# Residual gates and value products before the first output products, and GpSimd instead of SyncE as the issuer of the block-sum copies

## The chip, the cores and the metric

The kernel runs on one core of one Trainium2 chip. The metric is device time in microseconds of one execution. Engines are named as in the profile: PE is TensorE, PEld its weight loads, DVE is VectorE, ACT is ScalarE, POOL is GpSimd, SP is SyncE.

## The reference

An attention with two kinds of keys feeds a gated feed-forward layer. B = 4 batches, H = 8 heads, S = 768 positions, D = 64, blocks of 32 positions; the model width is 512, the inner width 1536.

```python
k_sum = k.reshape(B, H, nb, block, D).max(axis=3)      # one key per block of 32
v_sum = v.reshape(B, H, nb, block, D).mean(axis=3)     # one value per block
scores_l = scale * q @ k.T,  kept where |i - j| < 16
scores_s = scale * q @ k_sum.T + log(32)
a = softmax(concat(scores_l, scores_s))
x = a @ concat(v, v_sum)                               # heads side by side: 3072 x 512
g, val = x @ w_gate, x @ w_val
out = x + sigmoid(x @ w_res) * ((gelu(g) * val) @ w_out)
```

## The kernel before, in words

The work is cut into eight units of 384 rows; unit u is half `u % 2` of batch `u // 2`. A unit's attention is computed at the end of the unit before it, between that unit's output products, so PE has one long hand-written order of instructions.

**Attention.** Heads go in four pairs. `s_step` multiplies keys by queries: a tile of 64 queries meets 128 key rows, which are its own 64 positions, two rims of 16, the 24 block keys, and padding. ACT takes the exponential into `P` (L302, L299), and DVE multiplies `P` by the band mask `maskt` (L306); both factors of that product lie in SBUF. `av_step` multiplies `P` by `vext` (L320), which has the values in the same 128 rows: positions, rims, and in rows 96 to 127 the block means of v. DVE divides by the sum into `xn` (L338, L340). `xt_step` (PE and ACT, unit 0's end only) or `xt_dma` (SP, L350) turns `xn` into `xT`.

**Feed-forward.** For each of twelve slices `fo`, `fo_step` makes `g` and `vv` (L360), ACT the Gelu (L365), DVE the product into `gvT` (L366). They rotate through a PSUM pool of four banks, `ps_mm`, so `vv` of slice n waits until the DVE product of slice n-2 has been read. Then come the gate products `r` (`res_step`, L398, with a tanh on ACT, L401), the output products `f` (`ffn_step`, L408, three row blocks `sub` of twelve slices each), and `end_step` on DVE (L414, L417) with the store on SP (L421). `first_out` is the order of PE's work at the end of unit 0, `mid_out` that of units 1 to 6.

**Weights and the first unit.** POOL issues all loads of the beginning: gate and value weights in pieces, `w_res` (L193), two rims of v (L109, L110), then `w_out` in three pieces of four slices (L198). After these it issues batch 1's `k` and `v` (L103), and six loads of `q_nat`, 128 rows each (L123).

**Preparing the next batch.** In a batch's second unit its successor `nb` is prepared. `vsum_grp` makes block sums of v: twelve PE products into one bank (L258), a DVE copy into `vpart` (L262), four small DMAs of 6 rows each, from `vpart` into rows 96 to 119 of `vsum` (L264). `vsum_bc` then spreads `vsum` over the twelve tiles of `vext`: four POOL copies of three tiles each (L270). `turn_q` turns `q_nat` into `qT`, one DMA transpose on SP for each half batch (L132). SP and POOL each do their instructions in program order, so before the change SP reaches the two transposes behind the four small DMAs. In unit 1 this stands behind slice 4, in units 3 and 5 behind slice 1. In unit 1, `k` of batch 1 is turned by PE, and `k_place` puts reductions and copies on DVE at slices 0 to 3 (L222 to L231).

The later loads of k, v and q on POOL stand behind `pool_after`, a small copy that waits for the last `xT` of the unit, so they move with PE's work. The loads for batch 1 do not: they stand behind the loads of the beginning.

Of the kernel before, what the change touches and what calls it, by code (L numbers as in the profile page):

```python
# [15 lines left out]
def kernel(  # L16
# [11 lines left out]
    nc = tc.nc  # L28
# [14 lines left out]
    NSUB = TU // 128  # L43
# [35 lines left out]
    vsum = [const.tile([128, DM], BF16, name=f"vsum{i}") for i in range(2)]  # L79
# [50 lines left out]
    def turn_q(b, half):  # L130
        cs = slice(half * NSUB, (half + 1) * NSUB)
        nc.sync.dma_start_transpose(out=qT[b % 2][:, cs].rearrange("d c g k -> d (c g) k"),  # L132
                                    in_=q_nat[:, cs].rearrange("p c f -> p (c f)"))

    with tc.manual_schedule():
# [118 lines left out]
        def vsum_grp(b, pool, tag):  # L254
            vs = pool.tile([128, DM], F32, tag=tag, name="vs")
            for i in range(3):
                for g in range(4):
                    nc.tensor.matmul(vs[32 * g:32 * g + 32, :], bgrp[:, i, :],  # L258
                                     vext[b % 2][0:QT, 3 * g + i, :, 0:D],
                                     start=(i == 0), stop=(i == 2), tile_position=(0, 32 * g),  # L260
                                     skip_group_check=True)
            nc.vector.tensor_copy(vpart[:], vs[:])  # L262
            for g in range(4):
                nc.sync.dma_start(out=vsum[b % 2][96 + 6 * g:102 + 6 * g, :],  # L264
                                  in_=vpart[32 * g:32 * g + 6, :])

        def vsum_bc(b, lo, hi, eng):
# [21 lines left out]
        def s_step(u, hp, st, banks=None):  # L289
            if banks:  # L290
                s = [p.tile([128, 512], F32, tag=tag, name="s") for p, tag in banks]
            else:
                s2 = ps_s.tile([128, 2, 512], F32, tag="s", name="s")
                s = [s2[:, hh] for hh in range(2)]
            s_mm(u, hp, [x[:, 0:TU] for x in s])
            P = ppool.tile([128, 2, HT, QT], BF16, tag="P", name="P")
            if banks:
                for hh in range(2):
                    nc.scalar.activation(P[:, hh].rearrange("p t q -> p (t q)"), s[hh][:, 0:TU], AF.Exp,  # L299
                                         scale=scale, bias=bias_t[:])  # L300
            else:
                nc.scalar.activation(P.rearrange("p a t q -> p a (t q)"), s2[:, :, 0:TU], AF.Exp,  # L302
                                     scale=scale, bias=bias_t[:])
            if u:
                Pf = P.rearrange("p a t q -> p (a t) q")
                nc.vector.tensor_mul(Pf, Pf, maskt.unsqueeze(1).to_broadcast([128, 2 * HT, QT]))  # L306
            st["P", hp] = P
# [45 lines left out]
        def new_unit():  # L353
            return {"xn": upool.tile([128, KO, NSUB, 128], BF16, tag="xn", name="xn"),
                    "xT": upool.tile([128, KO, TU], BF16, tag="xT", name="xT")}
# [12 lines left out]
        def mm_tile(name):  # L368
            return ps_mm.tile([128, 512], F32, tag="mm", name=name)
# [24 lines left out]
        def res_step(st, sub):  # L394
            ss = slice(sub * 128, (sub + 1) * 128)
            r = mm_tile("r")
            for ko in range(KO):
                nc.tensor.matmul(r[:], st["xT"][:, ko, ss], w_res[:, ko, :],  # L398
                                 start=(ko == 0), stop=(ko == KO - 1))
            st["th", sub] = work.tile([128, DM], F32, tag="th", name="th")  # L400
            nc.scalar.activation(st["th", sub][:], r[:], AF.Tanh, scale=0.5)  # L401

        def ffn_step(st, gvT, sub, lo, hi):
            ss = slice(sub * 128, (sub + 1) * 128)
            if lo == 0:
                st["f", sub] = mm_tile("f")
            for fo in range(lo, hi):
                nc.tensor.matmul(st["f", sub][:], gvT[:, fo, ss], w_out[:, fo, :],  # L408
                                 start=(fo == 0), stop=(fo == FO - 1), skip_group_check=True)
# [13 lines left out]
        def end_step(u, st, sub):  # L423
            end_part(u, st, sub, st["f", sub], slice(0, DM))
# [28 lines left out]
        st = new_unit()  # L453
# [17 lines left out]
        gvT = upool.tile([128, FO, TU], BF16, tag="gvT", name="gvT")  # L471
# [49 lines left out]
        def first_out(u, st, gvT, nst):  # L521
            n = u + 1
            other = dict(pool=ps_t, tag="t")
            turn = dict(pool=ps_t, tag="t", copy=nc.scalar.copy)
            s_step(n, 0, nst)
            s_step(n, 1, nst, TO2)
            res_step(st, 0)
            res_step(st, 1)
            ffn_step(st, gvT, 0, 0, 4)
            av_step(n, 0, nst)  # L530
            av_step(n, 1, nst, **other)
            s_step(n, 2, nst)
            ffn_step(st, gvT, 1, 0, 4)
            res_step(st, 2)
            ffn_step(st, gvT, 2, 0, 4)
            xt_step(n, 0, nst, **turn)
            av_step(n, 2, nst)
            s_step(n, 3, nst)
            ffn_step(st, gvT, 0, 4, 8)
            ffn_step(st, gvT, 1, 4, 8)  # L540
            xt_step(n, 1, nst, **turn)
            ffn_step(st, gvT, 2, 4, 8)
            av_step(n, 3, nst)
            xt_step(n, 2, nst, **turn)
            ffn_step(st, gvT, 0, 8, FO)
            end_step(u, st, 0)
            ffn_step(st, gvT, 1, 8, FO)
            xt_step(n, 3, nst, **turn)
            ffn_step(st, gvT, 2, 8, FO)
            end_step(u, st, 1)  # L550
            end_step(u, st, 2)
# [36 lines left out]
        def pool_after(x):  # L588
            nc.gpsimd.tensor_copy(gate2[:], x)

        for u in range(NU):
            b, half = u // 2, u % 2
            nb = b + 1
            if half == 0 and nb == 1:
                k_sb[nb] = k_tile()
                load_k(nb, k_sb[nb], 0, 1)
                v_loads(nb)
                load_q_nat(nb)
            if u:
                gvT = upool.tile([128, FO, TU], BF16, tag="gvT", name="gvT")  # L600
            for fo in range(0 if u else 2, FO):
                if u > 1 and fo == 0:
                    fo_first(st, gvT)
                elif u and fo == FO - 2:
                    fo_last_two(st, gvT)
                elif u == 0 or fo < FO - 2:
                    fo_step(st, gvT, fo)
                if u == 0:
                    unit0_extras(fo)
                if u == 0 and fo == 9:  # L610
                    tq = turn_all(q_sb[1])
                if u == 0 and fo in (9, 10):
                    for hp in range(2 * fo - 18, 2 * fo - 16):
                        q_place(1, hp, tq[hp])
                if half == 0 and 1 < nb < B and fo == 0:
                    pool_after(st["xT"][0:1, KO - 1, 0:1])
                    k_nat = load_k_nat(nb)
                    v_loads(nb)
                if half == 0 and b and fo == 1:
                    v_rims(b, HT, NT)  # L620
                if half == 0 and 1 < nb < B and fo == 6:
                    turn_k(nb, k_nat)
                    k_rims(nb, slice(0, NP), nc.gpsimd)
                if half == 1 and nb < B:
                    if fo == 0:
                        v_rims(nb, 0, HT)
                        if nb > 1:
                            pool_after(st["xT"][0:1, KO - 1, 0:1])
                            load_q_nat(nb)
                    if fo == (4 if nb == 1 else 1):  # L630
                        vsum_grp(nb, ps_t, "t")
                        for i in range(4):
                            vsum_bc(nb, 3 * i, 3 * i + 3, nc.gpsimd)
                        turn_q(nb, 0)
                        turn_q(nb, 1)
                    if nb == 1:
                        if fo == 0:
                            tk = turn_all(k_sb[nb])
                        if fo < NP:
                            k_place(nb, fo, tk[fo])  # L640
                    elif 2 <= fo < 2 + NP:
                        k_blocks(nb, fo - 2)
            if u == NU - 1:
                last_out(u, st, gvT)
            else:
                nst = new_unit()
                (mid_out if u else first_out)(u, st, gvT, nst)
                st = nst
# [30 lines left out]
```

## Time and profile before

| | us |
|---|---|
| median of 6 runs | 261.24 |
| lowest and highest run | 260.77, 262.44 |
| the profiled execution, its own time | 262.18 |
| its span (first to last instruction) | 260.3 |
| PE busy | 250.0 |
| DVE busy | 156.7 |
| ACT busy | 126.0 |
| POOL busy | 104.1 |

The profiled execution took 1.88 us more than its span, and it stands 0.94 us above the median. The granted clock of PE was 0.999. Instructions that issue a DMA stand in the timeline of POOL or of SP's queue (SPq); the time to landing runs from the start of the issue. Unit 0 ends with `first_out` from about 40.2 to 55.7 us, unit 1 runs to 73.8 us, and the end of each later unit begins about every 28 to 29 us.

### The profile page before, as it was taken

The numbers are of one execution on the slowest core, as the hardware profiler recorded it, in microseconds if no ns is written. First come the engines' busy times: TensorE is split into PE (matmuls) and PEld (weight loads), VectorE is DVE, ScalarE is ACT, GpSimd is POOL, SyncE is SP. The second block draws the span as 40 slices with busy tenths as digits, with TensorE's granted clock in tenths as the row PEclk, the third lists the DMA queues.
The fourth block names the chain that finished last, engine by engine and source line by source line (L and its number), as shares of the span: only waits on it lengthen the run. The fifth ranks groups of instructions, "written<-read, shape, count | busy, mean of one in ns | idle before, by whom it ended". The sixth has DMA issues, their size and how long they took to land.

```text
span 260.3 us, 5828 instructions
## 1 busy us (share of the span) xinstructions
PE 250.0 (96%) x2306; PEld 138.3 (53%) x2306; DVE 156.7 (60%) x346; ACT 126.0 (48%) x210; POOL 104.1 (40%) x142
## 2 busy tenths in 40 slices
PE   6999987999999999999999999999999999999993
PEld 2565543555645565545654565545654665456543
DVE  5955653479668544677758444778566544854324
ACT  6785357456372535633383437443482337343310
POOL 8895454275080789234440888154530000000000
PEclk9999999999999999999999999999999999999999
DMA  5999999999962999949903999949904400230002
GB/s 82 177 116 180 197 220 195 198 130 196 67 121 48 173 136 139 128 119 167 149 8 64 191 113 145 115 118 172 150 12 114 100 0 3 48 137 0 0 37 86
DMA packets 98299, 29.61 MB, mean 114 GB/s; under 512 B 83384, under 2 KB 95104, under 8 KB 98160
## 3 DMA queue, kind: packets, MB, share of 16 engines
q0 software_dynamic: 68400, 14.96, 70.4%
q1 hardware_dynamic: 29872, 14.29, 24.7%
q8 instruction: 18, 0.29, 0.5%
q14 instruction: 9, 0.07, 0.1%
HBM read 29.36 MB, written 6.29 MB: 137 GB/s over the span
## 4 chain that ended last, share of the span: by engine, by line
PE 75%; DMA 14%; POOL 4%; DVE 3%; SPq 1%; issue 1%; ACT 0%; DVEq 0%
PE f L408 23%; PE g L360 19%; PE vv L360 19%; PE r L398 7%; DMA w_out<-in_moe_w_out_dram 5%; DMA w_gate<-in_moe_w_gate_dram 4%; DMA q_sb<-in_q_dram 3%; PE ao L320 3%; PE s L284 2%; DMA qT<-q_nat 2%; POOL vext L103 1%; POOL w_val L190 1%; POOL w_gate L189 1%; SPq L264 1%; DVE P L306 1%
## 5 line engine op out<-in xcount | busy, mean ns | idle before, releaser
L366 DVE TENSOR_TENSOR gvT<-ge,vv 128x384 bf16<-128x384 f32 x96 | 52.7, 552 | 51.6 <-PE vv L360 46.5
L365 ACT ACTIVATE ge<-g 128x384 f32<-128x384 f32 x96 | 47.1, 491 | 75.0 <-DVE gvT L366 41.4
L360 PE MATMUL g<-xT,w_gate 128*128 128x384 bf16 x384 | 78.8, 326 | 0.7 <-DMA w_gate<-in_moe_w_gate_dram 0.5
L360 PE MATMUL vv<-xT,w_val 128*128 128x384 bf16 x384 | 78.8, 326 | 0.7 <-DMA w_val<-in_moe_w_val_dram 0.7
L408 PE MATMUL f<-w_out,gvT 128*128 128x512 bf16 x276 | 64.9, 380 | 1.1 <-DMA w_out<-in_moe_w_out_dram 1.1
L360 PEld LDWEIGHTS <-w_gate 128*128 128x128 bf16 x384 | 37.1, 98 | 26.9 <-issue 1.6
L360 PEld LDWEIGHTS <-w_val 128*128 128x128 bf16 x384 | 37.2, 98 | 26.3 <-DMA w_val<-in_moe_w_val_dram 2.4
L408 PEld LDWEIGHTS <-gvT 128*128 128x128 bf16 x276 | 25.6, 98 | 30.5 <-DMA w_out<-in_moe_w_out_dram 1.6
L103 POOL DMA_DIRECT2D vext<-in_v_dram x48 | 32.6, 721 | 13.1 <-DMA w_out<-in_moe_w_out_dram 4.7
L401 ACT ACTIVATE th<-r 128x512 f32<-128x512 f32 x24 | 13.6, 606 | 28.4 <-PE r L398 28.4
L270 POOL COPY vext<-vsum 32x1536 bf16<-32x1536 bf16 x12 | 17.1, 1463 | 22.8 <-DMA vsum<-vpart 22.8
L414 DVE SCALAR_TENSOR_TENSOR th<-th,f 128x512 f32<-128x512 f32 (+2 forms) x26 | 16.7, 641 | 15.2 <-PE f L408 15.2
L306 DVE TENSOR_TENSOR P<-P,maskt 128x768 bf16<-128x768 bf16 x28 | 16.9, 605 | 11.8 <-ACT P L302 7.2
L398 PE MATMUL r<-w_res,xT 128*128 128x512 bf16 x96 | 23.2, 380 | 0.7 <-DMA w_res<-in_moe_w_res_dram 0.7
L302 ACT ACTIVATE P<-s,bias_t 128x768 bf16<-128x768 f32 x17 | 15.3, 902 | 7.1 <-PE s L284 6.9
L340 DVE TENSOR_TENSOR xn<-ao,rz 128x384 bf16<-128x384 f32 x32 | 17.8, 557 | 1.1
L417 DVE SCALAR_TENSOR_TENSOR o<-th,xn 128x512 f32<-128x512 f32 (+2 forms) x26 | 17.5, 674 | 1.5 <-DMA out_dram<-o 0.6
L117 POOL DMA_DIRECT2D k_nat<-in_k_dram x24 | 16.4, 745 | 1.1 <-DMA k_nat<-in_k_dram 0.8
L123 POOL DMA_DIRECT2D q_nat<-in_q_dram x18 | 15.9, 919 | 0.8 <-issue 0.7
L299 ACT ACTIVATE P<-s,bias_t 128x384 bf16<-128x384 f32 x30 | 15.7, 579 | 0.3 <-PE s L284 0.3
L222 DVE TENSOR_REDUCE ks<-kW 128x24 bf16<-128x768 bf16 x16 | 15.1, 944 | 0.4 <-ACT kW L237 0.3
L398 PEld LDWEIGHTS <-xT 128*128 128x128 bf16 x96 | 8.9, 98 | 10.6 <-issue 0.7
(82 smaller groups left out, 164.6 us busy)
## 6 DMA issues: line engine op xcount, KB each, us to landing
out_dram<-o SPq DMA_DIRECT2D x23, 256.0 KB, 2.3
vext<-in_v_dram POOLq DMA_DIRECT2D x48, 64.0 KB, 6.5
q_nat<-in_q_dram POOLq DMA_DIRECT2D x18, 128.0 KB, 7.4
w_gate<-in_moe_w_gate_dram POOLq DMA_DIRECT2D x6, 256.0 KB, 9.9
w_val<-in_moe_w_val_dram POOLq DMA_DIRECT2D x6, 256.0 KB, 10.5
w_out<-in_moe_w_out_dram POOLq DMA_DIRECT2D x3, 512.0 KB, 12.6
k_nat<-in_k_dram POOLq DMA_DIRECT2D x24, 64.0 KB, 4.6
vext<-vext SPq DMA_DIRECT2D x6, 144.0 KB, 5.7
```

The costliest lines, as they stand in the source:

```text
L103: nc.gpsimd.dma_start(out=vext[b % 2][0:QT, t, :, 0:D], in_=v[b, :, t * QT:(t + 1) * QT, :].rearrange("h p d -> p h d"))
L117: nc.gpsimd.dma_start(out=k_nat[:, t].rearrange("p (h d) -> p h d", d=D), in_=k[b, :, t * QT:(t + 1) * QT, :].rearrange("h p d -> p h d"))
L270: eng.tensor_copy(vext[b % 2][96:128, lo:hi, :, 0:D], src)
L306: nc.vector.tensor_mul(Pf, Pf, maskt.unsqueeze(1).to_broadcast([128, 2 * HT, QT]))
L340: nc.vector.tensor_mul(xn, ao[:, :, :, 0:D], rz.to_broadcast([128, NSUB, 2, D]))
L360: nc.tensor.matmul(ps[:, 0:TU], w[:, ko, fo * 128:(fo + 1) * 128], st["xT"][:, ko, :], start=(ko == 0), stop=(ko == KO - 1), skip_group_ch ...
L365: nc.scalar.activation(ge[:], g[:, 0:TU], AF.Gelu)
L366: nc.vector.tensor_mul(gvT[:, fo, :], ge[:], vv[:, 0:TU])
L398: nc.tensor.matmul(r[:], st["xT"][:, ko, ss], w_res[:, ko, :], start=(ko == 0), stop=(ko == KO - 1))
L408: nc.tensor.matmul(st["f", sub][:], gvT[:, fo, ss], w_out[:, fo, :], start=(fo == 0), stop=(fo == FO - 1), skip_group_check=True)
L414: nc.vector.scalar_tensor_tensor(th[:, cs], th[:, cs], 1.0, f[:, 0:n], ALU.add, ALU.mult)
L417: nc.vector.scalar_tensor_tensor(o.rearrange("p (k d) -> p k d", d=128), th[:, cs].rearrange("p (k d) -> p k d", d=128), 0.5, x, ALU.mult, ...
```

## The change

Three things are changed.

In `first_out` all three `res_step` stand together, ahead of the value products of head pairs 0 and 1 and the scores of pair 2. The first third of all three output products follows. Before, a third of output product 0 stood behind the second `res_step`, and the third `res_step` between output products 1 and 2.

The four DMAs from `vpart` to `vsum` are issued by POOL instead of SP, for batches 1, 2 and 3.

`turn_q` stands ahead of `vsum_grp` in the program. In unit 1 the block moves from slice 4 to slice 5. On POOL the four DMAs come behind the six loads of `q_nat` and ahead of the four copies; on SP the two transposes now follow the rims of v (L109, L110) directly.

```diff
@@ vsum_grp
             for g in range(4):
-                nc.sync.dma_start(out=vsum[b % 2][96 + 6 * g:102 + 6 * g, :],
+                nc.gpsimd.dma_start(out=vsum[b % 2][96 + 6 * g:102 + 6 * g, :],
                                   in_=vpart[32 * g:32 * g + 6, :])
@@ first_out
             s_step(n, 0, nst)
             s_step(n, 1, nst, TO2)
-            res_step(st, 0)
-            res_step(st, 1)
-            ffn_step(st, gvT, 0, 0, 4)
+            for sub in range(NSUB):
+                res_step(st, sub)
             av_step(n, 0, nst)
             av_step(n, 1, nst, **other)
             s_step(n, 2, nst)
-            ffn_step(st, gvT, 1, 0, 4)
-            res_step(st, 2)
-            ffn_step(st, gvT, 2, 0, 4)
+            for sub in range(NSUB):
+                ffn_step(st, gvT, sub, 0, 4)
             xt_step(n, 0, nst, **turn)
@@ main loop, half == 1 and nb < B
-                    if fo == (4 if nb == 1 else 1):
+                    if fo == (5 if nb == 1 else 1):
+                        turn_q(nb, 0)
+                        turn_q(nb, 1)
                         vsum_grp(nb, ps_t, "t")
                         for i in range(4):
                             vsum_bc(nb, 3 * i, 3 * i + 3, nc.gpsimd)
-                        turn_q(nb, 0)
-                        turn_q(nb, 1)
```

The number of instructions on PE, DVE and ACT is the same before and after.

## Prediction

> **What bounds the kernel now.** First the page, to see whose time counts.
>
> ```profile
> span 260.3 us, 5828 instructions
> PE 250.0 (96%) x2306; PEld 138.3 (53%) x2306; DVE 156.7 (60%) x346; ACT 126.0 (48%) x210; POOL 104.1 (40%) x142
> ```
>
> PE works 250.0 of 260.3 us, and the change takes no work from it. A gain can only come out of PE's pauses, so I looked for those near the edited lines. PE's timeline at the end of unit 0:
>
> ```profile
> 41.43 1.89 PE L398 MATMUL r<-w_res,xT 128*128 128x512 bf16 x8 [0.72 <-DMA w_res<-in_moe_w_res_dram]
> 44.38 1.04 PE L408 MATMUL f<-w_out,gvT 128*128 128x512 bf16 x4 [1.06 <-DMA w_out<-in_moe_w_out_dram]
> 45.35 0.57 PE L320 MATMUL ao<-vext,P 128*64 128x65 bf16 x24
> 45.85 0.35 PE L284 MATMUL s<-qT,kW 64*128 64x64 bf16 x12
> ```
>
> PE stands before the first output product until the first piece of w_out is there. Four r take 0.86 us in the chain, so eight that begin at 41.43 free PE at 43.16, and the pause in issue is 44.38 - 43.16 = 1.22 us (the row's 1.06 counts from the modelled end of the last r).
>
> The second place is the start of the attention for unit 2. The chain of waits there:
>
> ```profile
> 66.47 0.68 DVE vpart L262
> ...
> 69.46 0.66 SPq L264
> ...
> 70.29 3.96 DMA qT<-q_nat
> 74.25 0.04 issue
> 74.29 0.36 PE s L284 x12
> ...
> 75.61 2.34 DVE P L306 x2
> ```
>
> The scores wait for the turned q, whose transposes stood on SP behind four small DMAs, and those behind the copy into vpart. Then two mask products on DVE take 2.34 us. The timelines of DVE and POOL say why:
>
> ```profile
> 75.61 1.86 DVE L306 TENSOR_TENSOR P<-P,maskt 128x768 bf16<-128x768 bf16 x1 [1.04 <-ACT P L302]
> 77.40 0.55 DVE L306 TENSOR_TENSOR P<-P,maskt 128x768 bf16<-128x768 bf16 x1
> 104.40 0.56 DVE L306 TENSOR_TENSOR P<-P,maskt 128x768 bf16<-128x768 bf16 x1 [0.81 <-ACT P L302]
> ```
>
> ```profile
> 71.38 5.70 POOL L270 COPY vext<-vsum 32x1536 bf16<-32x1536 bf16 x4 [9.21 <-DMA vsum<-vpart]
> ```
>
> The same mask takes 0.56 us one unit later, with POOL idle, and 1.86 us here, where the last POOL copy runs until 77.08: it ends 0.4 us after that copy. The table of windows prices the whole, from the time when PE could begin the scores to its eleven-product f group:
>
> ```profile
> 73.84:78.77 4.93, 4.45 (x85) 2.53 (x85) 3.76 (x7) 3.49 (x7) 3.23 (x3) 1.00 0.34 64
> 102.85:106.96 4.11, 4.11 (x85) 2.36 (x85) 2.25 (x6) 3.48 (x7) 0.79 (x2) 1.00 1.74 143
> ```
>
> 4.93 against 4.11 us: 0.82 lost, 0.45 of it before the scores (74.29 - 73.84), 0.37 behind the masks.
>
> **Part one, the order at the end of unit 0.** In the pause go the third r (0.86, to 44.02), two value products (45.35 to 45.85: 0.50, to 44.52) and the scores of pair 2 (0.28, to 44.80). The first f then finds w_out landed (issued 32.37, 12.0 to landing, 44.37). What these need is there: the first two masks begin at 42.38 and 43.32 and take 0.56, so they end at 42.94 and 43.88; the rims of v land at 31.04 + 11.1 = 42.1; the exponentials that free the banks end at 43.28. ACT gets a third tanh (0.60) ahead of the exponential of pair 2, which starts about 44.9 instead of 46.24, for a value product near 47.6. The later pieces of w_out land at 34.35 + 12.6 = 46.95 and 35.67 + 13.8 = 49.47; PE now asks at 49.59 and 52.94, then 1.22 earlier. So unit 1 starts 1.22 us earlier. Cover gone, the price would be the pause again.
>
> **Part two, slice 5 instead of 4.** DVE is busy without pause from 58.8 to 68.1 and follows PE, so it moves 1.22 forward too. The block sums (12 products, 0.76 us from 63.87 to 64.64) used to separate vv of slices 4 and 5. Now vv 5 asks for its bank two groups of 0.65 behind vv 4, at 63.13 - 1.22 + 1.30 = 63.2, while the DVE product of slice 3 frees it at 64.74 - 1.22 = 63.5: about 0.3 us lost. Slice 6 has the sums ahead of it and waits no more. PE can begin the scores of unit 2 at 73.84 - 1.22 + 0.3 = 72.9. vpart, now behind the product of slice 5 (0.55), still ends about 66.4 instead of 67.15: the product of slice 4 ends at 66.02 + 0.54 - 1.22 = 65.3, and two operations follow that overlap a little.
>
> **Part three, the transposes ahead.** They wait for q_nat alone. Its third load has landed at 58.60 + 8.9 = 67.5, and a transpose lands 3.7 to 3.96 after its issue: 71.3 to 71.5. Unit 5's first transpose is issued while loads of q_nat still run and also takes 3.7. PE asks at 72.9, so the 0.45 us is gone, with 1.4 us in hand. The second transpose is for a later unit.
>
> **Part four, the small DMAs on POOL.** POOL idles for 9.21 us there, so the issues cost PE nothing by themselves; what counts is when the copies behind them end. A POOL issue of an SBUF-to-SBUF move takes 0.52 us (L109). Four from 66.45: the last starts at 68.0, ends at 68.5. From SP, the last issue ended at 70.12 and the copies began at 71.38, 1.26 later. The nearest POOL row with nothing ahead of it is a v load of 64 KB, 2.6 us from its start: 70.6. With 1.26 after the end it is 69.8. The four stand behind q_nat, whose last load lands at 61.20 + 8.1 = 69.3, so not earlier. I take 70.2, between the two, as the transfer is small but has loads ahead and the transposes beside it. Lower bound 69.5; upper 71.6, if each issue cost 0.94 like q_nat's (70.2 + 1.26 = 71.5).
>
> The Trainium skill, page "DMA: Bandwidth & Descriptors", section "Issuing engine by pattern", speaks against this part: plain copies belong on Sync, and its specifications give about 1 us to the first byte from GpSimd and 0.6 from Sync. By that page, an estimate, the copies would begin at 70.6 and the gain below would be 0.8.
>
> The copies take 5.70: they end at 75.9 instead of 77.08. PE's scores at 72.9 bring the first mask to DVE at 74.45 (104.40 - 102.85 = 1.55 later), inside the third or fourth copy. Even if it slips in between two copies, the second mask waits for the end of the last. In the trace before, the f group began 1.70 after POOL's end (78.77 - 77.07). So f begins at 75.9 + 1.70 = 77.6, against 78.77: **1.2 us earlier**. PE's own path allows 72.9 + 4.11 = 77.0, so 1.76 is the most.
>
> In batches 2 and 3, SP's small DMAs shared the queues with q_nat; the copies began 0.6 us after q_nat's last landing (unit 5: 177.77 + 6.8 = 184.5, then 185.15). On POOL they are right behind it. POOL ended its copies at s + 1.10 and s + 1.67 (133.01 - 131.91, 190.83 - 189.16), and by the mask rows PE loses only past s + 2.5, so I cost these at nothing. The cover is 1.4 and 0.8 us. All else in these units moves with xT.
>
> Sum: 262.18 - 1.2 = 261.0 for the profiled execution; the same difference on the median gives 261.24 - 1.2 = 260.0, told as 260.1 for small waits unseen.
>
> **The rivals.**
>
> Copies no longer in the way: if they begin by 69.6, PE's own path decides: 1.76 us, 259.5. For it: 1.26 after 68.5 is 69.8, close. Against: q_nat's landing at 69.3, and transposes that now run beside its last loads.
>
> The gain of unit 0 given back: if the copies begin between 70.6 and 71.38, the masks hand back what PE had won, and 0 to 0.78 stays: 260.5 to 261.2, centre 260.9. For it: four issues in a row, into a queue in use. Against: vpart is 0.75 us earlier and SP's four issues took 2.94 us, POOL's should take 2.1.
>
> Slower: the small DMAs, now in POOL's queue behind q_nat, land more than 2 us after it. The place is the masks of units 2, 4 and 6. Copies that begin at 72.4 cost 1.0 in unit 2; the same 1.9 behind the landing of q_nat instead of 0.6 costs 0.5 in unit 6 (1.3 less the cover of 0.8) and nothing in unit 4: 262.7. It decides from a start of 72.2 on, where the loss passes 0.78. For it: q_nat takes 8 us to land here, so this queue is long. Against: the rims from POOL (L109, L110) landed 0.3 to 0.5 us after the load ahead of them (41.8 and 42.1 behind w_res at 41.4).
>
> **How the numbers follow.** About 0.3% (0.78 us) is what a measurement of this kernel can tell from no change. Forecast 0.53; PE's own path 0.13; given back 0.23; slower 0.11. Faster is 0.53 + 0.13 = 0.66, of which 0.02 falls within 0.3%, as the forecast's lower end is near it: 0.64. Slower keeps 0.10, and 0.26 is left for no change. The range runs from 259.4, which takes in PE's own path, to 261.7, past no gain at all (261.24); outside lie most of the slower case, some 0.10, and about 0.05 for terms sized wrongly.
>
> **What would show it.** PE without a pause from r to the first f in unit 0, 12 output products in a row after the scores; unit 1 from about 54.5 us; PE at the scores of unit 2 by 72.9 without waiting for qT; POOL's copies from 70.2 and f about 77.6; the first mask in unit 2 still longer than 0.56; in units 4 and 6 masks of 0.56. The prediction is wrong if the copies begin at 71.4 or later, if masks in units 4 or 6 grow, or if a new wait for a PSUM bank appears at slice 5 that is much over 0.3 us.

## The result, and the profile after

The changed kernel takes 260.42 us (median of 21 runs, 259.78 to 261.44), the kernel before 261.52 (46 runs, 260.47 to 262.58). The ratio is 0.996, with a 95% interval from 0.9948 to 0.9972: faster by about 1.05 us, between 0.73 and 1.36.

The profiled execution of the changed kernel took 260.30 us. Its page begins:

```profile
span 258.4 us, 5826 instructions
PE 250.5 (97%) x2306; PEld 138.9 (54%) x2306; DVE 157.9 (61%) x346; ACT 125.9 (49%) x210; POOL 111.2 (43%) x154
```

The span is 1.9 us shorter, but PE's work is what it was (250.5 against 250.0), so all of it is pauses. Not all of them belong to the change, as the accounts below show. POOL has twelve instructions more: the small DMAs.

PE's timeline at the end of unit 0 (start, length, then what stood before it):

```profile
40.30 2.75 PE L398 MATMUL r<-w_res,xT 128*128 128x512 bf16 x12 [0.47 <-DMA w_res<-in_moe_w_res_dram]
42.98 0.57 PE L320 MATMUL ao<-vext,P 128*64 128x65 bf16 x24
43.76 2.76 PE L408 MATMUL f<-w_out,gvT 128*128 128x512 bf16 x12
...
53.32 0.81 PE L360 MATMUL g<-xT,w_gate 128*128 128x384 bf16 x4
```

The pause between r and f is gone, and f is a row of twelve without a wait. Unit 1 begins 13.02 us behind the first r, against 14.26 before (55.69 - 41.43): 1.24 us less.

The attention for unit 2, first in PE's timeline, then in the chain of waits:

```profile
71.47 0.52 PE L284 MATMUL s<-qT,kW 64*128 64x64 bf16 x24
...
76.36 0.38 PE L320 MATMUL ao<-vext,P 128*64 128x65 bf16 x12 [1.36 <-DVE P L306]
...
77.13 2.55 PE L408 MATMUL f<-w_out,gvT 128*128 128x512 bf16 x11
```

```profile
70.27 0.49 ACT ge L365
...
73.01 3.31 DVE P L306 x2
```

The scores wait for nothing any more: they follow the last vv at once, and SP's step, which stood in the chain, has left it. But the two masks are longer, 3.31 us instead of 2.34, and PE stands 1.36 us before the second half of the `ao` products. The timelines of DVE and POOL show them apart:

```profile
73.01 1.56 DVE L306 TENSOR_TENSOR P<-P,maskt 128x768 bf16<-128x768 bf16 x1 [0.81 <-ACT P L302]
74.50 1.81 DVE L306 TENSOR_TENSOR P<-P,maskt 128x768 bf16<-128x768 bf16 x1
```

```profile
65.71 2.02 POOL L264 DMA_DIRECT2D vsum<-vpart  x4 [3.94 <-DVE vpart L262]
71.29 6.35 POOL L270 COPY vext<-vsum 32x1536 bf16<-32x1536 bf16 x4 [3.56 <-DMA vsum<-vpart]
```

POOL issues the four small DMAs in 2.02 us, as forecast, then stands 3.56 us until the last has landed. The copies begin at 71.29 and lie under both masks, where before they lay under the first alone. The table of windows gives the price: the stretch from the scores of unit 2 to the first g of unit 2, and below it the same stretch for unit 3, where no copies run:

```profile
71.47:85.52 14.05, 12.69 (x146) 6.35 (x145) 10.36 (x18) 7.14 (x11) 7.09 (x7) 1.00 0.26 66
101.21:113.71 12.50, 12.50 (x146) 6.28 (x145) 8.20 (x18) 7.14 (x11) 2.21 (x5) 1.00 1.19 133
```

14.05 against 12.50: 1.55 us are lost here. Before, the same stretch (74.29 to 87.16) took 12.87.

So the two profiled executions differ by four items. The first r begins at 40.30 instead of 41.43 (1.13, the landing of `w_res`, ahead of everything edited); r to the first g of unit 1: 1.24 less; from there to the scores 18.15 instead of 18.60: 0.45 less; from the scores to the first g of unit 2: 1.18 more. The rest, from that g to the end, is 172.88 (258.4 - 85.52) instead of 173.14: 0.26 less. The sum, 1.13 + 1.24 + 0.45 - 1.18 + 0.26 = 1.90, is the difference of the spans. Without the first item, which changes from one execution to the next, 0.77 is left.

### The profile page after: what moved, and what is told of

Same layout as the page of the kernel before. It is cut to its first block, busy times and chain, and to the rows that moved or that the text cites. A ratio compares the mean times of both kernels' runs of the same rounds, so it can differ in the third digit from the quotient of the medians.

```text
span 258.4 us, 5826 instructions
## 1 busy us (share of the span) xinstructions
PE 250.5 (97%) x2306; PEld 138.9 (54%) x2306; DVE 157.9 (61%) x346; ACT 125.9 (49%) x210; POOL 111.2 (43%) x154
## 4 chain that ended last, share of the span: by engine, by line
PE 79%; DMA 12%; POOL 4%; DVE 2%; ACT 1%; issue 1%; POOLq 0%; DVEq 0%
PE f L408 23%; PE g L360 21%; PE vv L360 21%; PE r L398 8%; DMA w_res<-in_moe_w_res_dram 5%; DMA w_val<-in_moe_w_val_dram 3%; DMA q_sb<-in_q_dram 3%; PE ao L320 3%; PE s L284 2%; POOL vext L103 1%; DVE P L306 1%; POOL w_gate L189 1%; PE vs L258 1%; DMA out_dram<-o 1%; POOL w_val L190 1%
## 5 line engine op out<-in xcount | busy, mean ns | idle before, releaser
L360 PE MATMUL vv<-xT,w_val 128*128 128x384 bf16 x384 | 78.8, 326 | 0.5 <-DMA w_val<-in_moe_w_val_dram 0.5
L360 PE MATMUL g<-xT,w_gate 128*128 128x384 bf16 x384 | 78.8, 326 | 0.2
L306 DVE TENSOR_TENSOR P<-P,maskt 128x768 bf16<-128x768 bf16 x28 | 18.1, 648 | 11.5 <-ACT P L302 7.1
L270 POOL COPY vext<-vsum 32x1536 bf16<-32x1536 bf16 x12 | 17.7, 1517 | 13.1 <-DMA vsum<-vpart 13.1
(83 smaller groups left out, 173.1 us busy)
```

Source lines behind the costliest of these rows:

```text
L270: eng.tensor_copy(vext[b % 2][96:128, lo:hi, :, 0:D], src)
L360: nc.tensor.matmul(ps[:, 0:TU], w[:, ko, fo * 128:(fo + 1) * 128], st["xT"][:, ko, :], start=(ko == 0), stop=(ko == KO - 1), skip_group_ch ...
```

## The experiments

All of them compute the whole result. They use one account per profiled execution, in us, with the columns: start of the first r; r to the first g of unit 1; from there to the scores of unit 2; scores to the first g of unit 2 (12.50 where nothing is lost); from there to the end of the span. The last column is the ratio to the kernel before, with its interval.

| run | first r | to unit 1 | to scores | to unit 2 | to end | ratio |
|---|---|---|---|---|---|---|
| before | 41.43 | 14.26 | 18.60 | 12.87 | 173.1 | 1 |
| before again (e8) | 40.31 | 14.34 | 18.23 | 12.88 | 173.1 | - |
| changed | 40.30 | 13.02 | 18.15 | 14.05 | 172.9 | 0.9960 [0.9948, 0.9972] |
| changed again (e7) | 41.14 | 13.02 | 18.15 | 13.63 | 172.9 | 0.9956 [0.9940, 0.9973] |
| order alone (e1) | 40.80 | 13.03 | 18.41 | 12.86 | 173.1 | 0.9957 [0.9937, 0.9976] |
| queues alone (e2) | 40.72 | 14.24 | 18.14 | 13.88 | 172.8 | 1.0015 [0.9996, 1.0033] |
| changed, two copies late (e3) | 41.07 | 13.02 | 18.15 | 12.50 | 172.9 | 0.9946 [0.9926, 0.9966] |
| changed, small DMAs before the transposes (e4) | 40.73 | 13.03 | 21.06 | 12.50 | 172.8 | 1.0049 [1.0028, 1.0070] |
| order alone, two copies late (e5) | 40.58 | 13.03 | 18.51 | 12.49 | 173.5 | 0.9936 [0.9921, 0.9950] |
| changed, SP as issuer (e6) | 40.88 | 13.03 | 18.14 | 14.80 | 178.4 | 1.0136 [1.0108, 1.0163] |
| changed, slice 4 (e9) | 40.68 | 13.03 | 18.14 | 13.60 | 172.9 | 0.9964 [0.9943, 0.9985] |
| before, four more DMAs at the end (e10) | 40.38 | 14.50 | 18.69 | 12.82 | 172.9 | - |

### The two halves: the order alone, the queues alone

The first kernel is before with only the new order in `first_out`; the second is the changed kernel with the old order.

```diff
 e1: before, and of the change only
     first_out:  res_step x3 together, the three first ffn_step together
 e2: the changed kernel without that
```

> Part one alone: the new order of products at the end of unit 0, with the small block-sum DMAs left on SP, behind slice 4 and ahead of the transposes. Theory A (the pause ahead of the first output product is what the change removes, and DVE, the sums and POOL's copies follow PE): everything behind moves together by 1.2 us, so 261.5 - 1.2 = 260.3, about the whole change; PE still waits some 0.4 us for the turned q, and the masks of unit 2 are about as long as before (one of 1.9 us). Rival B (without the queue changes the copies stay where the loads of q put them and the masks hand the gain back): 0.3 to 0.6 us faster, 260.9 to 261.2, with the f group of unit 2 less than 0.6 us nearer to the start of the gate products.

> Parts two to four alone: the transposes ahead, the small DMAs on POOL, the block behind slice 5; the order at the end of unit 0 is the old one. Theory A: the 0.45 us that PE waited for the turned q goes, but the copy into vpart comes no earlier (67.2 to 67.7) and the small DMAs stand behind the first transpose, so POOL's copies begin at 71.5 to 72.2 and the masks take that back: within 0.5 us of before, 261.0 to 262.0. Rival B (the queues bring the gain): 0.8 us or more faster, at most 260.7.

Order alone: 260.30 us, ratio 0.9957, the whole gain of the changed kernel. POOL's and DVE's timelines:

```profile
69.32 5.70 POOL L270 COPY vext<-vsum 32x1536 bf16<-32x1536 bf16 x4 [7.47 <-DMA vsum<-vpart]
```

```profile
73.56 1.86 DVE L306 TENSOR_TENSOR P<-P,maskt 128x768 bf16<-128x768 bf16 x1 [0.86 <-ACT P L302]
```

With the small DMAs on SP the copies begin 28.5 us behind the first r (69.32 - 40.80), with POOL as issuer 31.0 (71.29 - 40.30). The first mask takes 1.86 and the second 0.55, as in the kernel before, and the loss there stays as small as it was (12.86).

Queues alone: 261.83 us, ratio 1.0015, where the interval just takes in no change. The timelines of PE, POOL and DVE:

```profile
73.10 0.52 PE L284 MATMUL s<-qT,kW 64*128 64x64 bf16 x24
```

```profile
72.76 6.35 POOL L270 COPY vext<-vsum 32x1536 bf16<-32x1536 bf16 x4 [3.54 <-DMA vsum<-vpart]
```

```profile
74.64 3.13 DVE L306 TENSOR_TENSOR P<-P,maskt 128x768 bf16<-128x768 bf16 x2 [0.81 <-ACT P L302]
```

The wait for the turned q is gone here too (18.14), and more is lost at the masks (13.88 instead of 12.87). What parts two to four give at q they hand back with interest at the masks. The time is inside what theory A allowed, but the copies begin at 72.76, later than its 71.5 to 72.2, although `vpart` ends at 66.88, before its 67.2.

### Is it the copies under the masks?

If the copies are what costs the 1.5 us, a kernel in which only two of them stand there must lose nothing. The second half of `vext` is needed only from unit 3 on, so copies 3 and 4 of batch 1 can go behind the loads of the next batch's k.

```diff
+                    if nb == 2:
+                        vsum_bc(1, 6, 9, nc.gpsimd)
+                        vsum_bc(1, 9, 12, nc.gpsimd)
...
-                        for i in range(4):
+                        for i in range(2 if nb == 1 else 4):
```

In e3 this is done to the changed kernel, in e5 to the kernel with the order alone, where the small DMAs are still on SP.

> The whole change, and in batch 1 the last two of POOL's four copies, which unit 3 alone reads, stand behind the loads of the next k instead of directly behind the first two. Theory A (what PE waits for in unit 2 is mask products that DVE cannot run while POOL copies): the copies end near 74.2 instead of 77.6, the second mask takes 0.56 us, the f group of unit 2 follows the scores by 4.1 to 4.3 us instead of 5.7, and the time is some 1.3 us below the changed kernel, 259.1. Rival (the masks are late for another reason, such as ACT's exponentials or the DMAs themselves): no change against the changed kernel, 260.4, and masks still over 1 us.

> Part one alone, and the last two of batch 1's four POOL copies behind the loads of the next k; the small DMAs stay on SP and ahead of the transposes. Theory A (part one brings 1.2 us, the masks 0.37, the turned q 0.45, each by itself): the masks no longer wait for the copies, PE still waits for the turned q; the f group of unit 2 follows the scores by 4.1 to 4.2 us and the time is 0.3 to 0.4 us below part one alone, 259.9. Rival (the masks' wait is hidden by something else): as part one alone, 260.3.

The timelines of POOL and DVE in e3:

```profile
71.72 2.87 POOL L270 COPY vext<-vsum 32x1536 bf16<-32x1536 bf16 x2 [3.74 <-DMA vsum<-vpart]
```

```profile
73.78 1.69 DVE L306 TENSOR_TENSOR P<-P,maskt 128x768 bf16<-128x768 bf16 x2 [0.81 <-ACT P L302]
```

POOL is done at 74.59, the first mask takes 1.22 us and the second 0.55, and the stretch is 12.50, with nothing lost: the copies under the masks were the whole loss. In e5 the copies end at 72.09, ahead of the masks, and both take 0.56 in DVE's timeline:

```profile
73.44 0.56 DVE L306 TENSOR_TENSOR P<-P,maskt 128x768 bf16<-128x768 bf16 x1 [0.82 <-ACT P L302]
74.38 0.56 DVE L306 TENSOR_TENSOR P<-P,maskt 128x768 bf16<-128x768 bf16 x1 [0.38 <-ACT P L299]
```

e5 took 259.86 us, ratio 0.9936 [0.9921, 0.9950], e3 259.68, ratio 0.9946 [0.9926, 0.9966]. They are the two fastest kernels of this study, and their intervals overlap, so which is better isn't settled. On one point e3 missed: its account promises 1.1 to 1.5 us over the changed kernel (12.50 against 13.63 and 14.05, with the other columns equal), but 0.3 to 0.4 came by the ratios, 0.7 by the medians (260.42 and 259.68). One profiled execution stands there for a median, and where the rest went is open.

### Why do the copies begin so late?

The four small DMAs were issued by 67.74 and the last landed at 71.24. Theory A says that the transposes, now ahead, hold them back; the rival, that this queue is slow behind the loads of q in any case. In e4 the transposes of batch 1 wait until the small DMAs have landed, by way of a 16-byte DMA on SP that reads `vsum`.

```diff
-                        turn_q(nb, 0)
-                        turn_q(nb, 1)
                         vsum_grp(nb, ps_t, "t")
+                        nc.sync.dma_start(out=scr[:], in_=vsum[1][119:120, 0:8])
+                        turn_q(nb, 0)
+                        turn_q(nb, 1)
```

(in unit 1; batches 2 and 3 as in the changed kernel)

> The whole change, but in batch 1 the two transposes wait, through a 16-byte DMA on SP that reads vsum, until the small DMAs have landed. Theory A (a running DMA transpose keeps the small DMAs of POOL's queue from being served): without a transpose under way the four land within 1.0 us of the last load of q_nat, as they do in units 4 and 6, so POOL's copies begin 0.6 to 1.2 us behind that landing instead of 2.4. PE then waits for the turned q until 73 to 74 us, so the time is 0.3 us faster to 0.5 us slower than the changed kernel. Rival (POOL's issue and its queue are slow by themselves): the copies still begin over 2 us behind q_nat's last landing, and the time is 1.5 us or more above the changed kernel, as the transposes come later too.

POOL's copies and PE's scores:

```profile
70.07 5.70 POOL L271 COPY vext<-vsum 32x1536 bf16<-32x1536 bf16 x4 [2.42 <-DMA vsum<-vpart]
```

```profile
74.82 0.53 PE L285 MATMUL s<-qT,kW 64*128 64x64 bf16 x24 [2.85 <-DMA qT<-q_nat]
```

Without transposes ahead POOL waits 2.42 us behind its last issue instead of 3.56, and the last small DMA takes 2.9 us from the start of its issue instead of 4.0. The DMA view of the same window, 67.3 to 69.4, first of the changed kernel, then of e4 (packets, MB, share; a packet's whole time counts where it starts, so a share can pass 100%):

```profile
q1 hardware_dynamic: 1086, 0.28, 125.6%
q0 software_dynamic: 2, 0.00, 0.1%
```

```profile
q0 software_dynamic: 154, 0.02, 11.1%
```

Queue q1 carries the transposes, q0 what POOL issues. In the changed kernel q0 moves two packets in 2.1 us while the transposes run; without transposes it moves 154. It is a stop and not an even slowing: from 66.4 to 67.3 q0 had moved 310 packets beside 214 of q1, and right after the stop, from 69.4 to 70.0, it moves again although the transposes go on:

```profile
q1 hardware_dynamic: 268, 0.06, 47.2%
q0 software_dynamic: 96, 0.02, 15.9%
```

Of the 24 rows of 1 KB that the small DMAs move, six go by 67.11, none until 69.58, and then 18 within 0.15 us. So in this order the transposes do hold the small DMAs back, for some 1.1 us (2.42 against 3.56). That settles the direction, not all of the size: A expected the copies 0.6 to 1.2 us behind the landing of the last q and the rival over 2; they begin 1.9 behind it (68.13 to 70.07), against 2.4 in the changed kernel. In e4 all 24 rows had moved by 68.4, and fifteen of the sixteen engines had reported the last small DMA done by 68.82, but the last only at 70.02. On one engine an instruction fetch stands in the DMA view in each kernel, here from 66.97 for 1.44 us. That the two are cause and effect wasn't tried.

Nor does every running transpose hold them back. A's expectation takes units 4 and 6 for places without one, but in unit 6 of the changed kernel the first transpose runs from 180.71 to 184.46, and the small DMAs land in the middle of it, by 183.43, 0.94 us behind q. There they had been issued 1.4 to 4.1 us ahead of the transpose; in unit 2 the first is issued within 0.1 us of it and the rest behind it. Whether that order makes the difference wasn't tried.

As a kernel e4 is slower: 262.97 us (nine runs, 261.81 to 263.49), ratio 1.0049 [1.0028, 1.0070]. That is over 1.5 us above the changed kernel, where the rival had it and not A: the scores wait 2.85 us for q, more than A had for it. The copies meet the masks no more (12.50).

### The transposes first, the small DMAs on SP

e6 is the changed kernel with part four undone: SP issues the small DMAs, behind the transposes.

```diff
-                nc.gpsimd.dma_start(out=vsum[b % 2][96 + 6 * g:102 + 6 * g, :],
+                nc.sync.dma_start(out=vsum[b % 2][96 + 6 * g:102 + 6 * g, :],
```

> The whole change but for the issuer: the small DMAs are issued by SP, now behind the two transposes. Theory A (a small DMA behind the transposes lands late, whoever issues it, and the copies decide unit 2): SP issues the four from about 70.5 on, the copies begin at 74.3 to 75.2, after both masks; the masks take 0.56 us, but the first value product waits for the second copy until 77.2 to 78.1, so the f group comes 0.8 to 1.7 us later than in the changed kernel: 261.2 to 262.1. Rival B (only POOL's queue is slow, SP's is not): the copies begin by 72.5 and the time is that of the changed kernel or less, 260.4.

265.58 us, ratio 1.0136 [1.0108, 1.0163]: 3.6 us slower than before. That is the median of four runs, 264.40 to 267.10. SP issues the small DMAs at 69.76 to 72.80 and the copies begin at 74.17, so early that the second mask still meets one (1.51 us instead of the expected 0.56). PE now waits for the copies themselves, in its timeline:

```profile
75.69 0.26 PE L320 MATMUL ao<-vext,P 128*64 128x65 bf16 x5 [0.42 <-POOL vext L270]
77.43 0.48 PE L320 MATMUL ao<-vext,P 128*64 128x65 bf16 x19 [1.49 <-POOL vext L270]
```

The expectation (261.2 to 262.1) counted unit 2 alone. The stretch from scores to g takes 14.80 there, 13.63 in unit 4 and 16.16 in unit 6, against 12.50. If `turn_q` is to stand ahead, the small DMAs must leave SP: part four is what makes part three bearable.

### Does the start of r move the loss? Slice 4 or 5?

e7 and e8 are the changed kernel and the one before, once more; e9 is the changed kernel with the block at slice 4.

> The changed kernel once more, for its time beside the others and for a second profile. Theory A (the start of r, set by the landing of w_res, differs by up to 1.1 us between executions, while the loads of q_nat, and with them the transposes, the small DMAs and the copies, do not move with it): whenever r begins, the f group of unit 2 begins at 77.0 to 77.4, so the distance from r to that f group is 36.8 where r begins at 40.3, and shorter by as much as r begins later. Rival (the distance is fixed by PE and DVE): 36.8 within 0.1 again, whenever r begins.

> The kernel before once more, for a second profile. Theory A (here the small DMAs and the transposes stand behind the copy into vpart, and so behind PE and DVE): the distance from the first r to the f group of unit 2 is 37.3 within 0.2, whenever r begins. Rival (the loads fix it here too): the f group at 78.8 within 0.2, whenever r begins.

> The whole change with the block of unit 1 back behind slice 4. The prediction priced the move to slice 5 at a wait of 0.3 us for a PSUM bank; the changed kernel's trace shows none. Theory A (the bank of that product was free anyway, and the copy into vpart comes between the products of slices 4 and 5, some 0.55 us earlier, in front of small DMAs that wait for the transposes): the same time as the changed kernel within 0.3 us, 260.4 to 261.0, vpart ending about 64.9 and the copies beginning within 0.4 us of 71.3 to 71.7. Rival (the move to slice 5 costs its 0.3 us in a way the trace does not show, or the earlier small DMAs pass the first transpose): 0.5 to 1.0 us faster than the changed kernel, the copies beginning at 70.5 or earlier.

The changed kernel came to 260.73 us again, ratio 0.9956. Its first r began 0.84 us later than in the first profile, the f group of unit 2 only 0.42 later (77.55 against 77.13; the record of its first product is missing, and 77.55 is counted back from the second). So in this kernel half of a late start is made up: the copies follow the loads of q, which follow the loads of the beginning, and a PE that comes later meets them less (the copies begin 0.60 us ahead of the scores instead of 0.18, and the stretch is 13.63 instead of 14.05). That lies between the two theories. In the kernel before, with r at 40.31, the stretch from the scores was the same as with 41.43 (12.88 and 12.87); the wait for q was 0.37 smaller. From r to the f group it took 37.06 (40.31 to 77.37, counted back in the same way), a little outside theory A's 37.3 within 0.2 and far from the rival, which had f at 78.8.

Slice 4: 260.24 us, ratio 0.9964, account as in e7. Part two is worth nothing that shows.

### A quarter of a microsecond at the end

From the first g of unit 2 to the end, the changed kernel is 0.25 us shorter with the same instructions on PE. What SP waits for at the very end, in the view of waits (line, releaser: total, count, mean), before and after:

```profile
SPq L674 <- DMA out_dram<-o: 1.1, 1, 1.1
```

```profile
SPq L672 <- DMA out_dram<-o: 0.8, 1, 0.8
```

At the end SP goes through eight DMA semaphores one by one, about 0.06 us each, and the last store sits on one of them: the second before, the sixth after, since twelve DMAs no longer come from SP. Then the program ends 1.29 and 1.03 us after the last landing. e10 is the kernel before with four 16-byte DMAs on SP in the last unit, which nothing reads; they shift the round by four.

```diff
+                for i in range(4):
+                    nc.sync.dma_start(out=scr[:, 8 * i:8 * i + 8], in_=maskt[0:1, 0:8])
```

> The kernel before with four 16-byte DMAs added on SP in the last unit, whose data nothing reads. They move the last store four places on in the round of eight semaphores, as the twelve small DMAs that left SP do in the changed kernel (12 fewer is the same place as 4 more). Theory A (after the last landing the program still goes through the semaphores behind the last store's one by one, 0.06 us each): the span ends 1.03 us after the last store lands, as in the changed kernel, instead of 1.29. Rival (the 0.25 us at the end come from something else in the change): 1.29 us as before. One look can't tell this by the total time, only by the end of the profile.

Its end came 1.05 us after the last landing, with the attention as before: the 0.25 us are the place of the last store in that round, and not the attention. It isn't the only thing that moves the end: e5 has the last store on the same place as before and ended 1.64 us after the landing; the 0.35 more stand behind the round, and their cause is open.

## Why the prediction was right, point by point

The forecast was 260.1 us, 1.2 below before; 1.05 came, with 1.2 inside its interval. The sum is right, but its reasons hold only for one part; that the rest came out near it is luck. Leaving out the start of r, and taking the mean of the two executions of each kernel, the account is: part one 1.28, the wait for q 0.27, the masks -0.97, the end 0.25, together 0.83. The rest of 1.05 is within the interval. Parts two to four were to come to nothing together (1.2 less 1.22); by the profiles they cost 0.45 (0.27 - 0.97 + 0.25), a loss that the medians of the changed kernel and of e1 (260.42 and 260.30) don't resolve.

**Part one, the order at the end of unit 0: right.** 1.22 forecast for the pause, 1.24 in the profiles (14.26 to 13.02), and e1 shows that this alone is the gain. The later pieces of `w_out` cause no wait. "Unit 1 from about 54.5" came out as 53.32 and 54.16, since r began 1.13 and 0.29 earlier; only the distance is a test.

**Part two, slice 5: a term too many.** The 0.3 us for a PSUM bank is 0: vv 5 follows its g without a gap at 62.06, while the DVE product of slice 3 ends at 62.53. In the trace its semaphore is one of ACT, so the bank it takes had been read by a Gelu; the prediction had it wait for the wrong reader. The kernel before has vv 5 wait for ACT as well, so its trace could have told this; the rule that `vv` of slice n waits for the DVE product of slice n-2 doesn't hold for slice 5. With the block at slice 4 (e9) the account is no other.

**Part three, the transposes ahead: right in the gain, wrong in what goes with it.** PE is at the scores at 71.47 without waiting. But the prediction timed a transpose at 3.7 to 3.96; the first one, beside the last load of q and the small DMAs, took 5.3 (65.65 to 70.92), which leaves 0.55 us in hand instead of 1.4. In e6, beside the same loads but with the small DMAs behind it, it took 4.0 (65.65 to 69.67). And it let the transposes cost the small DMAs little.

**Part four, the start of the copies: the term that failed.** Forecast 70.2, with bounds of 69.5 and 71.6; measured 71.29 and 71.71. In the first of these the last load of q had landed at 68.85 and not at 69.3, so the miss is larger than it looks. The issues were right (2.02 us for four). The rows that I used to price the landing, a v load and SP's own small DMAs, had no transposes beside them; e4 gives back 1.1 us when there are none. "The copies begin at 71.4 or later" was to refute the forecast, and in one of the two profiles they do. The step that failed is the 0.9 us (69.3 to 70.2) from the last q to the copies: it took 2.4.

The Trainium skill, page "DMA: Bandwidth & Descriptors", section "Issuing engine by pattern", puts plain copies on Sync, and the estimate by it, 70.6, was nearer than mine; the runs agree with the advice (e1's copies are 2.5 us earlier relative to r), though not by its latencies: it is the queue beside the transposes that costs. They agree only where the copies stand ahead of the transposes; behind them Sync was the worse issuer (e6, 265.58 us). The section "Queues, rings and completion order" of the same page has each DMA engine go round-robin between its queues packet by packet. By that a small DMA would pass beside the transposes; the 2 packets on q0 against 1086 on q1 in 2.1 us don't look like that, and for this stretch the measurement decides. Before and after it both queues move (310 and 214, 96 and 268 packets).

**From the copies to f: wrong, in the other direction.** "The second mask waits for the end of the last" copy, and f comes 1.70 after POOL's end. In the profile POOL ends at 77.64 and f begins at 77.13, before it. The masks slip in between the copies, and the copies that meet one take longer: 1.46 and 1.47, then 1.79 and 1.79 (the group took 6.35 instead of 5.70). By the prediction's rule f would have come at 71.29 + 5.70 + 1.70 = 78.7; it came 1.6 earlier. This error hid the one before it. The Trainium skill, page "SBUF — State Buffer", section "SBUF: two separate sides", says that a VectorE operation with two SBUF inputs and a GpSimd one that reads SBUF shut each other out for a whole instruction. The rows agree, 0.56 alone and 1.56 or 1.81 beside copies, and they show the consequence: which turn a mask gets between two copies decides between 0.4 and 1.5 us of loss. In the four profiles with POOL as issuer and all four copies in place (changed, e7, e2, e9; in e4 the masks come too late to meet a copy) the second mask ends 5.0 us behind the start of the copies, in front of the fourth's end, so the loss follows from how far ahead of the scores the copies begin: 0.18, 0.60, 0.34 and 0.63 us ahead give 14.05, 13.63, 13.88 and 13.60, always 14.23 less the lead within 0.01. In the kernel before, in e8 and in e1 the lead is 2.9 us, both masks end behind the last copy, and the stretch is 12.86 to 12.88.

**Units 4 and 6: right in the cost, not in the row.** The first masks took 0.72 and 0.62 us there instead of the 0.56 that I named, because the copies end at s + 1.85 and s + 1.75. PE lost nothing in either unit (12.49 from scores to g). "If masks in units 4 or 6 grow" was to refute the prediction and by the letter it did; but the kernel before has a mask of 0.74 in unit 6 in its second profile (e8), so this doesn't tell the two kernels apart.

**The rivals.** "Given back" had its premise met in one profile (copies from 71.29, inside its 70.6 to 71.38), and unit 2 did hand back 1.0 us; that the gain held all the same is due to the masks that slip between the copies, and to the end. "PE's own path" is what e3 and e5 come to, with two copies elsewhere. "Slower" had its premise partly right: the small DMAs land 2.4 us behind q, more than the 2 named, and the loss did come in unit 2, below its size; in units 4 and 6 they landed 0.99 and 0.94 behind q. None of them had the 0.25 us at the end.

## What to carry to other kernels

Test the parts of a change apart before believing its sum: here one part of four made the whole gain, and two errors in the others largely cancelled. When a transfer is moved to another queue, price it with what runs beside it in the new order, above all the transposes, and not by a row where that queue had the engines to itself. Where GpSimd copies and two-input DVE products share a stretch, look first whether some of the copies are needed there at all; moving half of them away took the loss to zero.

## What the hardware showed that was not expected

Small DMAs that POOL issues right behind the start of a DMA transpose can stand still beside it: 2 packets in 2.1 us, against 154 without transposes. It goes both ways: that transpose took 5.3 us, and 4.0 where the small DMAs came behind it (e6). In unit 6, issued ahead of the transpose, they landed beside it 0.94 us behind the last load.

An instruction fetch of 16 KB goes through the DMA engines of the kernel itself, in every version in unit 1. In the changed kernel it begins at 66.41 and holds one engine for 1.51 us, in the middle of the small DMAs and the transposes; in the DMA view from 66.4 to 67.9:

```profile
q8 instruction: 1, 0.02, 6.3%
```

A DMA split over sixteen engines ends with the last of them, and in e4 fifteen were done 1.2 us before the sixteenth. The traces show both facts and not that one causes the other. In e6 the fetch begins at 65.75, for 1.52 us, beside the same transpose, and there the transpose wasn't slow (4.0 us).

The end of a program depends by 0.25 us on which of eight semaphores the last store uses, 0.06 us for each step of the round.
